# Two edits to a fused retention, spectral and gated MLP kernel: the sign in the narrowing of weights, and seven block products in the first layer's u half

## The chip, the cores and the metric

The kernel runs on one core of a Trainium2 chip, in one launch. The time is device microseconds (us). A core has five engines with queues of their own: TensorE (PE in the rows; PEld is its weight load), VectorE (DVE), ScalarE (ACT), GpSimd (POOL), and SyncE (SP), which here only issues DMAs. An engine takes its instructions strictly in the order in which they were written for it, so an instruction that waits holds up all that stand behind it on that engine.

## The reference, cut to what matters

Two batches, 768 tokens, 512 features, everything in fp32. Retention with a decaying state gives x. Then:

```python
theta = x @ w_theta                                   # spectral part
y = w_tok_r @ (x*cos(theta)) + w_tok_i @ (x*sin(theta))   # over tokens
u = x + y
x2 = u + max(u @ w_ch, 0)
h = gelu_tanh(x2 @ w_in)                              # 512 -> 1024
u, v = h[..., :512], h[..., 512:]
v = layernorm(v) * g_ln
out = x2 + (u * (w_sg @ v + b_sg)) @ w_out            # w_sg over tokens
```

The weights of `w_theta`, `w_tok_*`, `w_ch`, `w_in` and `w_out` reach the kernel as 64-bit floats and are narrowed to fp32 on the chip.

## The kernel before, in words

The kernel keeps activations with features on the 128 partitions and tokens along the free axis. Tokens form three column groups g: group 0 is batch 0's first 512 tokens, group 1 is batch 1's, group 2 the last 256 of both. A feature tile e (or f, d) is one of four blocks of 128. So an activation tile is 128x512.

TensorE multiplies in a reduced format (fp32r), so each fp32 operand is split in a high and a low part (`split_hi` on ScalarE, `split_lo` on VectorE), and a product is made of three matmuls, high by high, low by high and high by low (`terms3`). A 512-deep layer for one output tile (`layer`, `up_v`) is therefore 4 x 3 = 12 matmuls of 128x512.

Twelve chunks of 128 tokens go through `retention` (scores, mask, outer product, state) and `theta` (angle, sine, cosine, transposes), then the token mixing (`mix_main`, `mix_rest`). After that come `channels` (w_ch), `up_v` and `up_u` (the two halves of w_in with `gelu`), `norm` and `norm_tile` (layer norm of v), `gate_tile` (w_sg), and the last layer. For groups 0 and 1 the last layer runs by Strassen and Winograd's scheme: its 2x2 blocks (two halves of the depth, two halves of the output, two groups) take seven block products in place of eight. `sum_weights` and `sum_tokens` form the sums and differences of blocks that it needs and split them, `seven` issues the products, and `finish_four` adds them up. One block product is 2 x 3 = 6 matmuls of 128x512, and there are two per scheme entry (j = 0, 1).

`weight(k)` loads 128x1024 64-bit words. Narrowing one takes: on ScalarE a Copy of the high words times 2^-112 (L403), on VectorE a right shift of the low words (L412), then two SCALAR_TENSOR_TENSOR operations (L423): the high words shifted left by three or-ed in, and the sign bit of the high words or-ed in. There are 19 weights. The first two (`W_THETA`) live in the homes of `xb` and `xa`; the others pass through two raw buffers.

The program's order is written out by hand: each operation is recorded with its engine, and the table `ORDER`, a list of the operations' numbers, with start times from a small planner, decides in which order each engine's instructions are emitted and which buffer each gets. Before TensorE's first real work, and in planned gaps, the kernel puts matmuls of zeros or of the identity, read from `state` and `ident` (`keep_warm`). Their results are not used.

Of the kernel before, what the change touches and what calls it, by code (L numbers as in the profile page):

```python
# [10 lines left out]
F32 = mybir.dt.float32  # L11
# [20 lines left out]
REBIAS = 2.0**-112  # L32

# [29 lines left out]
class Plan:  # L63
# [160 lines left out]
def retention_spectral_gmlp(  # L224
# [153 lines left out]
    def weight(k, prio, eng=dve, after=()):  # L378
# [19 lines left out]
        def words(hi):  # L398
# [5 lines left out]
                out=words(1).bitcast(F32), in_=words(1).bitcast(F32), func=AF.Copy, scale=REBIAS  # L404
# [15 lines left out]
        for scalar, op in ((3, ALU.logical_shift_left), (-0x80000000, ALU.bitwise_and)):  # L420
            dve(
                1024,
                lambda scalar=scalar, op=op: V.scalar_tensor_tensor(  # L423
                    out=words(0), in0=words(1), scalar=scalar, in1=words(0),
                    op0=op, op1=ALU.bitwise_or,
                ),
                prio=prio,
                r=[(raw, 1)],
                w=[(raw, 0)],
            )  # L430
# [408 lines left out]
    def channels(g, e, prio):  # L839
# [9 lines left out]
        dve(512, relu, ps=True, r=[t], w=x_keys(g, e), prio=prio)  # L849
        split_x(x2hl, g, e, prio)  # L850

    def gelu(t, o, prio):

        s = Buf()
        act(
# [561 lines left out]
```

## Time and profile before

| | us |
|---|---|
| median of 3 runs | 370.33 (369.91 to 370.38) |
| the profiled execution, its own time | 370.23 |
| its span, first to last instruction | 368.5 |
| TensorE busy | 363.0 |
| VectorE busy | 290.1 |
| ScalarE busy | 178.6 |
| the PE part of the chain of work that ended last | 95% of the span |

The span is what the rows show, and 1.7 us of the execution's time lies around it. Busy time of an engine is the union of its instructions. The chain of work that ended last goes back from the last instruction, at each step to what released it, so its pieces add up to the span.

### The profile page before, as it was taken

Reading aid. Unit: us, or ns where it says so; the run is one execution under the profiler, and the core shown is the slowest. Engines: PE = TensorE matmul, PEld = TensorE weight load, DVE = VectorE, ACT = ScalarE, POOL = GpSimd, SP = SyncE. Lnnn points to the kernel's source line nnn. Section 1 sums busy time; section 2 is a strip of 40 time slices with the busy share of each in tenths; the row PEclk is TensorE's granted clock in tenths of the full one; section 3 lists DMA queues with packets and bytes.
Section 4 is the critical chain, followed back from the end, with each engine's and each line's share of the span. In section 5 each row is a group of like instructions: output and inputs, shape, how many; then the busy total and the mean of one; then the engine's idle time right before and its main releaser. Section 6 shows DMA issues by size and latency. Waiting matters only on the chain.

```text
span 368.5 us, 5764 instructions
## 1 busy us (share of the span) xinstructions
PE 363.0 (99%) x2364; PEld 311.7 (85%) x2364; DVE 290.1 (79%) x441; ACT 178.6 (48%) x298; POOL 10.8 (3%) x18
## 2 busy tenths in 40 slices
PE   8899999999999999999999999999999999999996
PEld 7788888788998988889988888888888889988885
DVE  3999999998886885775786434897999596899984
ACT  2767987742543566634343212437493744314300
POOL 1021010030001000000000000000000000000000
PEclk9999999999999999999999999999999999999999
DMA  7999990233433121414160000000000000000134
GB/s 306 410 413 407 410 384 6 88 141 121 166 114 116 34 84 34 166 30 161 68 223 6 2 0 0 2 1 0 0 2 0 0 2 1 3 0 2 58 114 171
DMA packets 10346, 39.08 MB, mean 106 GB/s; under 512 B 1360, under 2 KB 2384, under 8 KB 7888
## 3 DMA queue, kind: packets, MB, share of 16 engines
q1 hardware_dynamic: 10176, 38.67, 27.7%
q8 instruction: 18, 0.29, 0.3%
q10 hardware_dynamic: 144, 0.05, 0.1%
q14 instruction: 8, 0.07, 0.1%
HBM read 35.57 MB, written 3.15 MB: 105 GB/s over the span
## 4 chain that ended last, share of the span: by engine, by line
PE 95%; DMA 4%; DVE 0%; SPq 0%; issue 0%
PE banks L311 93%; DMA b<-qkv 3%; PE banks L716 1%; DMA dec<-decays 1%; DVE b L1231 0%; SPq L457 0%
## 5 line engine op out<-in xcount | busy, mean ns | idle before, releaser
L311 PE MATMUL banks<-b,b 128*128 128x512 f32 (+2 forms) x1776 | 327.3, 351 | 0.0
L311 PEld LDWEIGHTS banks<-b,b 128*128 128x128 f32 (+1 forms) x1776 | 276.4, 183 | 46.0 <-issue 1.2
L331 ACT ACTIVATE b<-b 128x512 fp32r<-128x512 f32 (+1 forms) x71 | 56.0, 815 | 67.4 <-DVE b L423 23.5
L337 DVE TENSOR_TENSOR b<-b,b 128x512 fp32r<-128x512 f32 (+1 forms) x71 | 62.4, 898 | 15.4 <-ACT b L331 9.2
L423 DVE SCALAR_TENSOR_TENSOR b<-b 128x1024 int32<-128x1024 int32 x32 | 38.8, 1224 | 0.8 <-ACT b L403 0.3
L331 ACT ACTIVATE b<-xa 128x512 fp32r<-128x512 f32 (+1 forms) x26 | 17.1, 670 | 25.4 <-DVE xa L845 15.9
L403 ACT ACTIVATE b<-b 128x1024 f32<-128x1024 f32 x16 | 18.6, 1160 | 11.6 <-DMA b<-wts 8.6
L857 ACT ACTIVATE b<-banks 128x512 f32<-128x512 f32 x24 | 13.7, 589 | 15.0 <-PE banks L311 15.0
L337 DVE TENSOR_TENSOR b<-xa,b 128x512 fp32r<-128x512 f32 (+1 forms) x26 | 19.1, 743 | 1.7 <-ACT b L331 1.6
L311 PE MATMUL banks<-b 64*128 64x128 f32 (+1 forms) x352 | 19.3, 256 | 0.8 <-DMA b<-qkv 0.8
L875 ACT ACTIVATE b<-b 128x512 f32<-128x512 f32 x24 | 14.7, 625 | 10.8 <-DVE b L865 10.8
L311 PEld LDWEIGHTS banks<-b 64*128 64x128 f32 (+1 forms) x352 | 17.1, 165 | 3.0 <-DMA b<-qkv 1.1
L865 DVE SCALAR_TENSOR_TENSOR b<-b,banks 128x512 f32<-128x512 f32 x24 | 15.9, 680 | 4.1 <-ACT b L857 4.1
L881 DVE SCALAR_TENSOR_TENSOR b<-b,banks 128x512 f32<-128x512 f32 x24 | 16.4, 682 | 2.6 <-ACT b L875 2.5
L724 DVE TENSOR_TENSOR b<-banks,b 128x1024 f32<-128x1024 f32 x12 | 14.7, 1223 | 3.9 <-ACT b L707 2.2
L526 ACT ACTIVATE b<-b,dec 128x64 f32<-128x64 f32 x56 | 14.1, 335 | 7.4 <-DMA b<-qkv 7.4
L503 DVE TENSOR_TENSOR b<-banks,causal 128x512 f32<-128x512 f32 x24 | 15.8, 686 | 1.7 <-PE banks L311 1.7
L412 DVE TENSOR_SCALAR b<-b 128x1024 int32<-128x1024 int32 x16 | 11.4, 717 | 4.2 <-DMA b<-wts 4.2
L331 ACT ACTIVATE b<-xb 128x512 fp32r<-128x512 f32 (+1 forms) x13 | 8.4, 663 | 12.3 <-DVE xb L845 8.7
L1036 DVE SCALAR_TENSOR_TENSOR b<-banks,gcol,brow 128x512 f32<-128x512 f32 x12 | 8.9, 749 | 5.5 <-PE banks L311 5.5
L845 DVE SCALAR_TENSOR_TENSOR xa<-banks,xa 128x512 f32<-128x512 f32 x8 | 5.5, 690 | 8.0 <-PE banks L311 7.9
L311 PE MATMUL banks<-b,state 64*64 64x128 f32 x160 | 10.9, 275 | 0.0
(66 smaller groups left out, 193.2 us busy)
## 6 DMA issues: line engine op xcount, KB each, us to landing
b<-wts SPq DMA_DIRECT2D x16, 1024.0 KB, 4.9
b<-qkv SPq DMA_DIRECT2D x24, 512.0 KB, 11.1
out<-b SPq DMA_DIRECT2D x11, 256.0 KB, 2.1
b<-wsg SPq DMA_DIRECT2D x9, 256.0 KB, 7.0
xa<-wts SPq DMA_DIRECT2D x2, 1024.0 KB, 11.2
xb<-wts SPq DMA_DIRECT2D x1, 1024.0 KB, 8.3
brow<-bvec SPq DMA_DIRECT2D x1, 384.0 KB, 11.4
dq<-qdecays SPq DMA_DIRECT2D x1, 256.0 KB, 6.4
```

The lines of the kernel that those rows point to most:

```text
L311: nc.tensor.matmul(out=o, lhsT=l, rhs=r, start=start, stop=stop, skip_group_check=more)
L331: act(words, lambda: A.activation(out=hi(), in_=src(), func=AF.Copy), prio=prio, r=r, **k)
L337: lambda: E.tensor_tensor(out=lo(), in0=src(), in1=hi().bitcast(F32), op=ALU.subtract),
L403: lambda: A.activation(out=words(1).bitcast(F32), in_=words(1).bitcast(F32), func=AF.Copy, scale=REBIAS),
L423: lambda scalar=scalar, op=op: V.scalar_tensor_tensor(out=words(0), in0=words(1), scalar=scalar, in1=words(0), op0=op, op1=ALU.bitwise_or,),
L503: V.tensor_tensor(out=ap(at[i])[:, h * 512 + lo : h * 512 + hi].rearrange("p (n t) -> p n t", n=n), in0=ap(sc[h])[:, lo:hi].rearrange("p ( ...
L526: A.activation(out=v, in_=v, func=AF.Copy, scale=dk[:, h : h + 1])
L724: V.tensor_tensor(out=z2, in0=ap(tp)[:, None, :].to_broadcast([P, 2, 512]), in1=z2, op=ALU.mult)
L857: lambda: A.activation(out=ap(s), in_=ap(t), func=AF.Square),
L865: lambda: V.scalar_tensor_tensor(out=ap(s), in0=ap(s), scalar=1.0 / GA, in1=ap(t), op0=ALU.add, op1=ALU.mult),
L875: lambda: A.activation(out=ap(s), in_=ap(s), func=AF.Tanh, scale=GA * GC),
L881: lambda: V.scalar_tensor_tensor(out=ap(o), in0=ap(s), scalar=1.0, in1=ap(t), op0=ALU.add, op1=ALU.mult),
```

## The change

There are two edits, and with them a new order.

The narrowing: ScalarE's Copy becomes a parametric relu with the same scale and alpha = 2^32. A negative word is so multiplied by a further 2^32, which sets one bit of its exponent field; the left shift by three moves that bit to the sign's place. The second SCALAR_TENSOR_TENSOR goes.

The first layer: the u half of w_in for groups 0 and 1 (eight layers of 12 matmuls) is now formed by `seven` as well, with a new function `up_four` that adds up the parts and calls `gelu`. Group 2 keeps `up_u`. `sum_weights` and `sum_tokens` are called for it.

```diff
-                out=words(1).bitcast(F32), in_=words(1).bitcast(F32), func=AF.Copy, scale=REBIAS
+                out=words(1).bitcast(F32), in_=words(1).bitcast(F32), func=AF.Prelu, scale=REBIAS,
+                alpha=SIGN_UP,
...
-        for scalar, op in ((3, ALU.logical_shift_left), (-0x80000000, ALU.bitwise_and)):
-            dve(
-                1024,
-                lambda scalar=scalar, op=op: V.scalar_tensor_tensor(
-                    out=words(0), in0=words(1), scalar=scalar, in1=words(0),
-                    op0=op, op1=ALU.bitwise_or,
-                ),
+        dve(
+            1024,
+            lambda: V.scalar_tensor_tensor(
+                out=words(0), in0=words(1), scalar=3, in1=words(0),
+                op0=ALU.logical_shift_left, op1=ALU.bitwise_or,
+            ),
...
+    def up_four(j, ws, ts, prio):
+        z, x, y, u, v = seven(W_INU, x2hl, ws, ts, j, prio)
+        for g, f, part in ((0, j, z), (1, j, x), (0, 2 + j, y), (1, 2 + j, v)):
...
+                t = v if part is v else Buf()
+                dve(
+                    512,
+                    lambda t=t, part=part: V.tensor_tensor(
+                        out=ap(t), in0=ap(part), in1=ap(u), op=ALU.add
+                    ),
...
+            gelu(t, gu[g, f], prio, ps=part is z)
...
+    ws = sum_weights(W_INU, t - 8)
+    ts = sum_tokens(lambda g, d: (lambda: x_tile(g, d), x_keys(g, d)), t - 4)
+    for f in range(NP):
+        up_u(2, f, t)
+    for j in range(2):
+        up_four(j, ws, ts, t)
...
 ORDER = [
-    56, 58, 57, 85, 86, 59, 0, 114, 113, 60, 141, 142, 63, 62, 64, 61, 741, 87, 66, 7, 90, 88, 169,
+    48, 50, 49, 78, 77, 51, 105, 106, 0, 52, 161, 133, 55, 54, 56, 53, 189, 82, 57, 58, 134, 79, 6,
...
```

The whole of `ORDER` is new (972 operations in place of 935). Three places of it matter below.

First, TensorE at the program's start, before: scores, outer products and attend of chunks 0 to 2. `ident` rows are the unused matmuls; the rows begin behind chunk 0's scores; b_100, b_108 and b_121 hold q and k of chunks 1 to 3, b_98, b_102 and b_106 k and v of chunks 0 to 2; b_126 and b_166 are masked scores; 128x512 rows are the first angle.

```order
L311 MATMUL banks<-ident 128x128 x2
L311 MATMUL banks<-b_98 64x64 x8
L311 MATMUL banks<-b_100 128x128 x8
L311 MATMUL banks<-b_126,b_98 64x128 x8
L311 MATMUL banks<-ident 128x128 x2
L716 MATMUL banks<-ident,xa_86 128x128 x4
L311 MATMUL banks<-b_102 64x64 x8
...
L311 MATMUL banks<-b_108 128x128 x8
L311 MATMUL banks<-b_106 64x64 x8
L311 MATMUL banks<-b_121 128x128 x8
...
L311 MATMUL banks<-b_235,b_179 128x512 x2
```

The same place now. Here b_102, b_105, b_123, b_121 and b_139 hold q and k of chunks 1, 2, 3, 4 and 5, and b_100 and b_107 k and v of chunks 1 and 2.

```order
L314 MATMUL banks<-ident 128x128 x2
L314 MATMUL banks<-b_98 64x64 x8
L314 MATMUL banks<-ident 128x128 x2
L314 MATMUL banks<-b_126,b_98 64x128 x8
L314 MATMUL banks<-b_102 128x128 x8
L314 MATMUL banks<-b_100 64x64 x8
L314 MATMUL banks<-b_105 128x128 x8
...
L314 MATMUL banks<-b_121 128x128 x8
L719 MATMUL banks<-ident,xa_86 128x128 x8
L314 MATMUL banks<-b_123 128x128 x8
L314 MATMUL banks<-b_139 128x128 x8
L314 MATMUL banks<-b_269,b_173 128x512 x2
```

Two more scores and one more chunk's transposes now stand ahead of the first angle. On SP's queue the first weight (xb) moved from sixth to eighth, behind both loads of chunk 2, and `gcol` and four gate weights went from among the first 33 loads to later places.

Second, VectorE between the channel tiles and the first layer, before (L845 is the relu of a channel tile, L337 a low part).

```order
L845 SCALAR_TENSOR_TENSOR xa_87<-banks,xa_87 128x512
L337 TENSOR_TENSOR b_1873<-xb,b_1873 128x512
L337 TENSOR_TENSOR b_1855<-xb,b_1855 128x512
L412 TENSOR_SCALAR b_1834<-b_1834 128x1024
L845 SCALAR_TENSOR_TENSOR xa_86<-banks,xa_86 128x512
```

And now, where L848 is the relu, L1098 a difference of token blocks, and L340 a low part.

```order
L848 SCALAR_TENSOR_TENSOR xa_87<-banks,xa_87 128x512
L1098 TENSOR_TENSOR b_1913<-xa_87,xa_86 128x512
L848 SCALAR_TENSOR_TENSOR xa_86<-banks,xa_86 128x512
L1098 TENSOR_TENSOR b_1928<-xa_87,b_1913 128x512
L340 TENSOR_TENSOR b_1857<-xb,b_1857 128x512
L1098 TENSOR_TENSOR b_1931<-xa_87,xa_86 128x512
L340 TENSOR_TENSOR b_1875<-b_1557,b_1875 128x512
L340 TENSOR_TENSOR b_1946<-b_1931,b_1946 128x512
L340 TENSOR_TENSOR b_1948<-b_1913,b_1948 128x512
L848 SCALAR_TENSOR_TENSOR xa_86<-banks,xa_86 128x512 x2
```

The differences stand among the channel tiles' relus; b_1948 and b_1946, the low parts of the first difference of blocks, are what the first of the seven products reads. On TensorE those products follow the channel tiles of groups 1 and 0; the four channel tiles of group 2 follow the first two products.

Third, VectorE between the last layer norm (it ends with L955, now L958) and the gate tiles, before.

```order
L955 SCALAR_TENSOR_TENSOR rstd<-mv,rstd 128x4
L865 SCALAR_TENSOR_TENSOR b_2515<-b_2515,banks 128x512
L881 SCALAR_TENSOR_TENSOR b_2552<-b_2452,banks 128x512
L881 SCALAR_TENSOR_TENSOR b_2552<-b_2515,banks 128x512
L1075 TENSOR_TENSOR b_2556<-b_1834,b_1780 128x512
L337 TENSOR_TENSOR b_2580<-b_2343,b_2580 128x512
```

And now.

```order
L958 SCALAR_TENSOR_TENSOR rstd<-mv,rstd 128x4
L340 TENSOR_TENSOR b_2592<-b_2420,b_2592 128x512
L340 TENSOR_TENSOR b_2597<-b_2420,b_2597 128x512
L340 TENSOR_TENSOR b_2152<-b_1483,b_2152 128x512
L340 TENSOR_TENSOR b_2465<-b_2273,b_2465 128x512
L340 TENSOR_TENSOR b_2434<-b_2268,b_2434 128x512
L1039 SCALAR_TENSOR_TENSOR b_2691<-banks,gcol_75,brow 128x512
L340 TENSOR_TENSOR b_2662<-b_2594,b_2662 128x512
L340 TENSOR_TENSOR b_2667<-b_2594,b_2667 128x512
L340 TENSOR_TENSOR b_2695<-b_2565,b_2695 128x512
L340 TENSOR_TENSOR b_2671<-b_2565,b_2671 128x512
```

The last four rows are group 1's normalised v, low parts, behind a row that reads the third gate tile of group 0 (L1039). On TensorE the last `up_v` of group 1 now stands directly ahead of group 0's four gate tiles; before, six layers of `up_u` stood between. Group 2's first gate tile follows group 0's four and is the first to read those low parts.

## Rows read from the trace of the kernel before

**Rows 1.** The page: busy time, and TensorE's granted clock in 40 slices, in tenths.

```profile
PE 363.0 (99%) x2364; PEld 311.7 (85%) x2364; DVE 290.1 (79%) x441; ACT 178.6 (48%) x298; POOL 10.8 (3%) x18
...
PEclk9999999999999999999999999999999999999999
```

**Rows 2.** The chain that ended last, in order of time: start, us, what.

```profile
16.56 30.70 PE banks L311 x384
...
49.68 8.20 PE banks L311 x36
...
130.49 234.79 PE banks L311 x1188
...
365.30 0.42 DVE b L1231
```

**Rows 3.** Timeline of TensorE from 4 to 19 us: start, duration, what.

```profile
4.80 1.16 PE L311 MATMUL banks<-b 64*128 64x128 f32 x16
5.89 0.71 PE L311 MATMUL banks<-ident 128*128 128x128 f32 x4
6.66 1.78 PE L311 MATMUL banks<-b 128*64 128x64 f32 x32
...
9.39 0.71 PE L311 MATMUL banks<-ident 128*128 128x128 f32 x4
10.26 0.66 PE L716 MATMUL banks<-ident,xa 128*128 128x128 f32 x4 [0.15 <-DVE xa L622]
10.84 0.69 PE L311 MATMUL banks<-b 128*64 128x64 f32 x16
...
13.50 0.49 PE L311 MATMUL banks<-ident 128*128 128x128 f32 x2
14.15 1.78 PE L311 MATMUL banks<-b 64*128 64x128 f32 x32 [0.16 <-DMA b<-qkv]
16.56 1.16 PE L311 MATMUL banks<-b 64*128 64x128 f32 x16 [0.64 <-DMA b<-qkv]
```

**Rows 4.** Timeline of all engines from 6 to 18 us.

```profile
6.52 1.28 DVE L503 TENSOR_TENSOR b<-banks,causal 128x512 f32<-128x512 f32 x2
8.47 2.02 ACT L526 ACTIVATE b<-b,dec 128x64 f32<-128x64 f32 x8 [5.97 <-DMA b<-qkv]
11.57 1.20 ACT L403 ACTIVATE xb<-xb 128x1024 f32<-128x1024 f32 x1 [0.56 <-DMA xb<-wts]
12.80 2.91 DVE L423 SCALAR_TENSOR_TENSOR xb<-xb 128x1024 int32<-128x1024 int32 x2
15.75 1.14 ACT L331 ACTIVATE b<-xb 128x1024 fp32r<-128x1024 f32 x1 [0.88 <-DVE xb L423]
17.42 1.22 DVE L337 TENSOR_TENSOR b<-xb,b 128x1024 fp32r<-128x1024 f32 x1
```

**Rows 5.** Groups by line and shape: count, busy us, mean ns, idle before.

```profile
L423 DVE SCALAR_TENSOR_TENSOR b<-b 128x1024 int32<-128x1024 int32 x32 | 38.8, 1224 | 0.8 <-ACT b L403 0.3
L337 DVE TENSOR_TENSOR b<-b,b 128x512 fp32r<-128x512 f32 x43 | 28.6, 686 | 5.3 <-ACT b L331 5.3
L331 ACT ACTIVATE b<-b 128x512 fp32r<-128x512 f32 x43 | 25.7, 623 | 30.8 <-DVE b L1043 16.0 <-DVE b L1095 9.2 <-PE banks L311 4.0
L311 PEld LDWEIGHTS banks<-b,b 128*128 128x128 f32 x1584 | 266.2, 189 | 44.2 <-ACT b L526 0.3
L1332 ACT ACT_TABLE_LOAD x1 | 1.3, 1283 | 1.2 <-PEq L1407 1.2
L966 ACT ACTIVATE b<-b,rstd 128x512 f32<-128x512 f32 x12 | 9.5, 807 | 2.3 <-DVE rstd L955 2.3
L954 DVE SCALAR_TENSOR_TENSOR rstd<-rstd 128x4 f32<-128x4 f32 x9 | 1.5, 162 | 0.3
```

**Rows 6.** Busy time of each engine by stretch (PE, PEld, DVE, ACT, ...).

```profile
17.00:60.00 43.00, 43.00 (x445) 36.30 (x441) 41.69 (x56) 34.02 (x73) 4.94 (x4) 1.00 0.90 360
...
130.00:240.00 110.00, 110.00 (x563) 94.32 (x562) 71.19 (x95) 45.66 (x67) 0.00 (x0) 1.00 0.17 61
```

More of the change, by code (lines that the diff above doesn't have):

```diff
@@ L32 @@
 REBIAS = 2.0**-112
+SIGN_UP = 2.0**32
 W_THETA, W_MAIN, W_REST, W_CH, W_INV, W_INU, W_OUT = 0, 2, 8, 11, 13, 15, 17
@@ L419, in weight @@
         )
-        for scalar, op in ((3, ALU.logical_shift_left), (-0x80000000, ALU.bitwise_and)):
-            dve(
-                1024,
-                lambda scalar=scalar, op=op: V.scalar_tensor_tensor(
-                    out=words(0), in0=words(1), scalar=scalar, in1=words(0),
-                    op0=op, op1=ALU.bitwise_or,
-                ),
[L427 to L430, printed above, removed]
+        dve(
[4 more added lines that the diff above has]
+            ),
+            prio=prio,
+            r=[(raw, 1)],
+            w=[(raw, 0)],
+        )
         h, l = wp[k]
@@ L850, in channels, with gelu @@
         split_x(x2hl, g, e, prio)
-    def gelu(t, o, prio):
+    def gelu(t, o, prio, ps=True):
         s = Buf()
@@ L857, in gelu @@
             lambda: A.activation(out=ap(s), in_=ap(t), func=AF.Square),
-            ps=True,
+            ps=ps,
             r=[t],
@@ L867, in gelu @@
             ),
-            ps=True,
+            ps=ps,
             r=[t],
@@ L883, in gelu @@
             ),
-            ps=True,
+            ps=ps,
             r=[t, s],
@@ L1104, in sum_tokens, with seven @@
         return res
-    def seven(base, src, hl, ws, ts, j, prio):
+    def seven(base, hl, ws, ts, j, prio):
         z, w, x, y = (bank() for _ in range(4))
@@ L1172, in store @@
         dma(256, put, r=[o], prio=prio)
+    def up_four(j, ws, ts, prio):
+        z, x, y, u, v = seven(W_INU, x2hl, ws, ts, j, prio)
+        for g, f, part in ((0, j, z), (1, j, x), (0, 2 + j, y), (1, 2 + j, v)):
+            if f % 2 == 0:
+                gu[g, f], gu[g, f + 1] = halves()
+            t = part
+            if part is not z:
+                t = v if part is v else Buf()
[4 more added lines that the diff above has]
+                    ),
+                    ps=part is not v, r=[part, u], w=[t], prio=prio,
+                )
+            gelu(t, gu[g, f], prio, ps=part is z)
     def finish_four(j, ws, ts, prio):
-        z, x, y, u, v = seven(W_OUT, None, ghl, ws, ts, j, prio)
+        z, x, y, u, v = seven(W_OUT, ghl, ws, ts, j, prio)
         def add(o, a, b, r, **k):
@@ L1269, in retention_spectral_gmlp @@
         weight(W_INU + k, t - 10 + 5 * k)
-        weight(W_INV + k, t - 7 + 5 * k)
+        weight(W_INV + k, t + 30 + 5 * k)
     for g in range(3):
@@ L1274, in retention_spectral_gmlp @@
             t += 2.7
+    ws = sum_weights(W_INU, t - 8)
+    ts = sum_tokens(lambda g, d: (lambda: x_tile(g, d), x_keys(g, d)), t - 4)
+    for f in range(NP):
+        up_u(2, f, t)
+        t += 2.7
+    for j in range(2):
+        up_four(j, ws, ts, t)
+        t += 9.5
     for g in (0, 2, 1):
@@ L1281, in retention_spectral_gmlp @@
             norm_tile(g, q, t + 1)
-        for f in range(NP):
-            up_u(g, f, t)
-            t += 2.7
     dma(384, lambda: nc.sync.dma_start(out=brow, in_=bvec), w=["brow"], prio=t - 20)
@@ L1296, in retention_spectral_gmlp @@
         weight(W_OUT + k, t + 20 + 5 * k)
-    for g in (2, 0, 1):
+    for g in (0, 2, 1):
         for f in range(NP):
```

96 rows, old and new, of the table ORDER are left out of this document.

## The prediction

> **What bounds the kernel now.** I read the page first, then the chain that ended last, then TensorE's timeline at the start and last the busy time by stretch. TensorE is busy for 363.0 of 368.5 us at a granted clock of 1.0, its higher level of 2.4 GHz, in every slice [rows 1]. Busy alone proves little, so the chain decides: from 16.56 us to its last matmul at 365.3 it runs along TensorE and names no wait on another engine, and only 0.42 us of VectorE follows [rows 2]. A stretch of it gives the price of one matmul: 36 of 128x512 in 8.20 us, 227.8 ns each [rows 2]. VectorE is at 41.69 of 43 us from 17 to 60 us, but TensorE did not wait for it; from 130 to 240 us it has 38.8 of 110 us to spare [rows 6]. So time goes in three ways only: fewer matmuls, less waste before 16.56, or new waits.
>
> Before 16.56 TensorE is not full. The unused matmuls of the identity and the DMA waits show it: real work ends at 5.89 and goes on at 6.66, ends at 9.39 and goes on at 10.26, 13.50 to 14.15, and 15.93 (14.15 + 1.78) to 16.56 [rows 3]. That is 0.77 + 0.87 + 0.65 + 0.63 = 2.92 us without real work.
>
> **The change part by part.** *The products.* Eight layers of 12 matmuls go, and 14 block products of 6 come: 96 - 84 = 12 matmuls of 128x512 less, 12 x 227.8 ns = 2.73 us [rows 2]. TensorE is the chain, so this comes off the end, if nothing new waits.
>
> Each of these matmuls has its own weight load, of 189 ns on average, and PEld is busy for 85% of the span [rows 1, 5]. The Trainium skill (Perfetto Trace Analysis, Identifying the Most-Contended Engine) says that matmul occupancy is no good measure of how near TensorE is to its peak and that the weight loads' busy share is. By the loads the 12 matmuls would give 12 x 189 ns = 2.27 us in place of 2.73. I go by the start-to-start spacing, which holds the load and whatever else paces a matmul.
>
> *VectorE's third operation.* 19 operations of 1224 ns go, 23.3 us [rows 5]. Most stand in the stretch in which VectorE is full, but TensorE waits for none of them after 16.56, so directly they give nothing. What they do give is freedom at the start (next point). Prelu in Copy's place: the trace shows no Prelu. The nearest row, Copy with a scale, takes 1.20 us [rows 4]; I take the same, bounds 0.6 less and 1.2 more (a second pass). ScalarE is idle about half the time, and the first weight below has 0.6 us of room, so even the upper bound costs some 0.6 us once.
>
> *What `up_four` adds.* On VectorE: 4 weight sums and 4 low parts, 8 token sums and 8 low parts, 4 adds in `both`, 6 adds in `up_four`: 34 x 0.686 = 23.3 us, what the narrowing gave back, but now between 130 and 240 us, into 38.8 us of idle time [rows 5, 6]. On ScalarE 4 + 8 high parts and 4 copies: 16 x 0.62 = 10 us into 64 us of idle time there. The `gelu` passes only change where they read. Cost on the path: zero, if the operands of the products are early enough. The tightest place is the first product. Its two operands' low parts stand six passes behind the relu of the second channel tile of group 0 (third pair of order rows, its second place). That tile ends two channel tiles, 2 x 12 x 0.228 = 5.5 us, before the product; relu and six passes are 7 x 0.63 = 4.4 us (two masks in a row took 1.28 [rows 4]), so about 1 us of room. Behind it four channel tiles of group 2, 10.9 us, cover the rest: 19 passes, 12 us, up to the latest operand of the next products, less the 1 us of room ahead and 2.7 us of the two first products. I take 0; bounds 0 and 3 us.
>
> *The start.* The order puts the first weight's load behind chunk 2's two loads, and more chunk work ahead of the first angle. Landings before: the fourth load by 8.4, the weight (after 256 KB for dq) by 11.57, two loads later 14.15, then 16.56 [rows 3, 4]: 2.55 us for 1 MB, and one step of 2.41 us for 0.5 MB. So now q and k of chunk 1 land at 8.4, of chunk 2 at 10.3, its k and v at 11.6, the weight at 14.1, chunk 4's q and k between 15.4 and 16.5, then one load per 1.3 us. TensorE: scores 0 as before to 5.89; the same 0.77 us until VectorE has faded v; outer product to 7.3; attend 0 needs both masks, which end at 6.52 + 1.28 = 7.80, so 0.6 us of filler; from 7.9 attend 0 (1.0), scores 1 (1.1), outer 1 (0.5), scores 2 (1.1, its data landed at 10.3), attend 1 and 2 (2.05 each), outer 2 (0.5) follow with their data there, to 16.3. Then scores 4, a wait of 0 to 0.2 us. Waste 0.77 + 0.6 + 0.1 = 1.5 us for 2.92 us: gain 1.4 us. Behind it come transposes of two chunks and scores 3 and 5, to 20.4 us, when the first angle starts. Is the weight there? Landed 14.1, Prelu 1.2, one operation of 1.46 (half of 2.91), high part 1.14, low part about 1.22 [rows 4] make 19.2, and about 0.6 us of VectorE's other passes stand between: 19.8, so 0.6 us early. With the second operation it would be 21.3 and late by 0.9: this is where the removed operation pays. Bounds of this term: a gain of 1.9 us (waste 1.0) and a loss of 1 us (the slow load step falls ahead of the weight and Prelu takes two passes). Behind it the loads stay ahead: one chunk load per 1.3 us against some 4 us of work per chunk.
>
> *The rest.* Switches between shapes change in number by a few, each some 0.1 to 0.2 us by the attend and score rows; I take 0, bounds 0.3 either way. The tail behind the last matmul, 0.42 us of VectorE and the store, has the same code.
>
> Sum against the profiled execution: 370.23 - 2.73 - 1.4 = 366.1 us. That execution lies 0.10 us under the median of 370.33, so the same figure serves for the median.
>
> **The rivals.** *The start gives nothing (367.5 us).* If the first angle waits for its weight or for a load, only the products remain: 370.23 - 2.73 = 367.5. For it: the room is 0.6 us, less than the slow load step of 1.1 us beyond the normal pace. Against: scores of three later chunks stand ahead and take up such a slip.
>
> *The last normalisation is late (368 to 370 us).* The last `up_v` of group 1 now ends where group 0's four gate tiles begin, 4 x 18 x 0.228 = 16.4 us before group 2's gate tile that reads it; before, six layers, 16.4 us more, lay between. Its path: gelu four passes, statistics and Newton steps of 14 x 0.162, together about 6 us, ScalarE's four scalings with high parts 4 x (0.81 + 0.62) = 5.7 [rows 5], then low parts that stand behind a row that reads the third gate tile, done at 12.3: 12.5 + 0.7 + 4 x 0.63 = 15.7. Room 0.7 us, and 2 more for batch 1's second half of that tile. If VectorE is 2 to 4 us late, as it may be with other work between, TensorE waits that long: 368 to 370.
>
> *The sums are in the way (371.7 us).* Slower than before. If the token and weight sums do not run beside the channel tiles but behind the last of groups 0 and 1, then 24 passes, 24 x 0.686 = 16.5 us, meet a cover of 10.9 us, and TensorE waits 5.6 us at the first layer's second set of products: 366.1 + 5.6 = 371.7. It decides from the point where the passes ahead of the products take more than those 10.9 us. For it: strict order on VectorE, where a relu that waits for TensorE holds up the sums behind it. Against: half of the sums stand ahead of the last relu.
>
> *Prelu forces table loads (372.5 us).* The one table load of the trace took 1.283 us [rows 5]. If Prelu were not in the loaded set, each narrowing would need a load there and one back, 2.57 us. From 17 to 60 us ScalarE is busy 34.0 of 43 us and narrows five weights: 34.0 + 12.8 = 46.8, some 4 us over; with 2.57 us at the first weight, 6.4 us, so 372.5. The Trainium skill (ScalarE: Activation LUTs, Table sets: the hidden batching unit) states that functions are loaded as sets and names copy and relu, not the parametric relu, among those that come with every set. Against: the built program still has one table load, ahead of all activations, as the trace of before has.
>
> **How the numbers follow.** Forecast, both gains within 0.8 us: 0.63 (365.3 to 366.9). Start without gain: 0.14. Late normalisation: 0.14, of which 0.05 end above 369.6. Sums in the way: 0.05. Table loads: 0.04. About 0.2%, 0.74 us, is what a measurement of this kernel can tell from no change. So faster 0.63 + 0.14 + 0.09 = 0.86, same 0.05, slower 0.09. The range reaches from 365.2 (gains of 2.73 and 1.9 and 0.3 for switches) to 368.8, which takes in the start without gain and the smaller half of the late normalisation.
>
> **What would show it.** Right: 1116 matmuls of 128x512 in place of 1128 at the same spacing; the chain on TensorE from about 16.5 us on without a wait; the first angle near 20.4 us, with six scores and two chunks' transposes ahead of it; one table load; Prelu near 1.2 us; VectorE fuller from 130 to 240 us and emptier from 17 to 60. Wrong: a wait of TensorE on a low part ahead of the first angle, at the first layer's products, or at group 2's first gate tile, or a spacing other than 228 ns.

## The result, and the profile after

The changed kernel takes 366.85 us (median of 4 runs, 366.21 to 367.32) against 370.32, a ratio of 0.9908, 95% interval 0.989 to 0.9925. It is faster by 3.5 us; the forecast was 366.1 in a range from 365.2 to 368.8. The profiled execution took 367.32 us with a span of 365.6, so it is the slowest of the four. Over all eight runs (four more stand below) the median is 366.5.

The page of the changed kernel, its busy line, answers to [rows 1]: VectorE as busy as before, ScalarE 7.9 us more, 14 matmuls fewer.

```profile
PE 361.2 (99%) x2350; PEld 310.4 (85%) x2350; DVE 290.6 (79%) x456; ACT 186.5 (51%) x314; POOL 12.4 (3%) x18
```

The chain that ended last (start, us, what) answers to [rows 2]. Its pace is the same, 8.20 us for 36 matmuls, and no wait stands in it from the first matmul on.

```profile
56.66 8.20 PE banks L314 x36
...
150.75 211.66 PE banks L314 x1080
...
362.43 0.42 DVE b L1251
```

The groups by line and shape (count, busy us, mean ns, idle before), answering to [rows 5]. 1116 matmuls of 128x512 instead of 1128. Prelu (now L406) takes 1153 ns for 1024 words, and there is one table load.

```profile
L314 PE MATMUL banks<-b,b 128*128 128x512 f32 x1116 | 258.1, 391 | 0.0
L426 DVE SCALAR_TENSOR_TENSOR b<-b 128x1024 int32<-128x1024 int32 x16 | 19.5, 1220 | 0.5 <-ACT b L406 0.3
L406 ACT ACTIVATE b<-b 128x1024 f32<-128x1024 f32 x16 | 18.4, 1153 | 11.0 <-DMA b<-wts 11.0
L1357 ACT ACT_TABLE_LOAD x1 | 1.3, 1283 | 1.2 <-PEq L1432 1.2
```

Busy time by stretch (PE, PEld, DVE, ACT, ...), answering to [rows 6]: VectorE went from 41.69 to 37.75 us in the first and from 71.19 to 82.98 in the second.

```profile
17.00:60.00 43.00, 43.00 (x478) 36.28 (x475) 37.75 (x51) 35.36 (x75) 6.05 (x5) 1.00 0.68 272
...
130.00:240.00 110.00, 110.00 (x580) 94.06 (x579) 82.98 (x117) 54.48 (x84) 0.12 (x1) 1.00 0.14 51
```

TensorE's timeline at the start (start, duration, what) answers to [rows 3]. Here is the one surprise.

```profile
3.96 1.49 PE L314 MATMUL banks<-ident 128*128 128x128 f32 x6
5.37 2.08 PE L314 MATMUL banks<-b 64*128 64x128 f32 x16
7.38 0.71 PE L314 MATMUL banks<-ident 128*128 128x128 f32 x4
...
9.27 1.09 PE L314 MATMUL banks<-b,b 128*64 128x128 f32 x16
...
19.77 2.06 PE L314 MATMUL banks<-b 64*128 64x128 f32 x32
21.75 3.04 PE L314 MATMUL banks<-b,b 128*128 128x512 f32 x12
```

The first scores take 2.08 us where they took 1.16 [rows 3]. The profile's record of TensorE's clock begins, at 1.0, at 7.31 us of this span and at 4.12 us of the span of before; ahead of that point identity matmuls start 0.213 us apart, behind it 0.111, so it is the step from 1.2 to 2.4 GHz. The first angle (the first 128x512 matmuls) starts at 21.75 us, forecast 20.4. From there to VectorE's last pass is 362.43 - 21.75 = 340.68 us; before it was 365.30 - 19.70 = 345.60.

### The profile page after: what moved, and what is told of

The parts are those of the page before. It is cut to its first block, busy times and chain, and to the rows that moved or that the text cites. A ratio compares the mean times of both kernels' runs of the same rounds, so it can differ in the third digit from the quotient of the medians.

```text
span 365.6 us, 5779 instructions
## 1 busy us (share of the span) xinstructions
PE 361.2 (99%) x2350; PEld 310.4 (85%) x2350; DVE 290.6 (79%) x456; ACT 186.5 (51%) x314; POOL 12.4 (3%) x18
## 4 chain that ended last, share of the span: by engine, by line
PE 99%; DVE 0%; issue 0%
PE banks L314 97%; PE banks L719 1%; DVE b L1251 0%; DVE state L272 0%; DVE halfpi L276 0%
## 5 line engine op out<-in xcount | busy, mean ns | idle before, releaser
L334 ACT ACTIVATE b<-b 128x512 fp32r<-128x512 f32 (+1 forms) x83 | 62.6, 786 | 51.9 <-DVE b L1098 17.0
L340 DVE TENSOR_TENSOR b<-b,b 128x512 fp32r<-128x512 f32 (+1 forms) x83 | 70.2, 870 | 14.5 <-PE banks L314 8.9
L406 ACT ACTIVATE b<-b 128x1024 f32<-128x1024 f32 x16 | 18.4, 1153 | 11.0 <-DMA b<-wts 11.0
L340 DVE TENSOR_TENSOR b<-xa,b 128x512 fp32r<-128x512 f32 (+1 forms) x26 | 18.7, 728 | 4.9 <-ACT b L334 4.9
L426 DVE SCALAR_TENSOR_TENSOR b<-b 128x1024 int32<-128x1024 int32 x16 | 19.5, 1220 | 0.5 <-ACT b L406 0.3
L529 ACT ACTIVATE b<-b,dec 128x64 f32<-128x64 f32 x56 | 14.1, 334 | 5.4 <-DMA b<-qkv 5.4
L684 DVE SCALAR_TENSOR_TENSOR b<-banks,b 128x512 f32<-128x512 f32 x12 | 8.3, 689 | 7.9 <-PE banks L314 4.8
L675 ACT ACTIVATE b<-banks 128x512 int32<-128x512 f32 x12 | 7.1, 590 | 14.3 <-PE banks L314 14.3
L969 ACT ACTIVATE b<-b,rstd 128x512 f32<-128x512 f32 x12 | 9.6, 808 | 8.5 <-DVE rstd L958 8.5
L884 DVE SCALAR_TENSOR_TENSOR b<-b,banks 128x512 f32<-128x512 f32 x18 | 12.2, 680 | 1.7 <-ACT b L878 1.3
L868 DVE SCALAR_TENSOR_TENSOR b<-b,banks 128x512 f32<-128x512 f32 x18 | 11.9, 679 | 1.0 <-ACT b L860 0.9
L860 ACT ACTIVATE b<-banks 128x512 f32<-128x512 f32 x18 | 10.4, 593 | 4.5 <-PE banks L314 3.7
```

Of the source, the lines that this page charges most:

```text
L334: act(words, lambda: A.activation(out=hi(), in_=src(), func=AF.Copy), prio=prio, r=r, **k)
L340: lambda: E.tensor_tensor(out=lo(), in0=src(), in1=hi().bitcast(F32), op=ALU.subtract),
L406: lambda: A.activation(out=words(1).bitcast(F32), in_=words(1).bitcast(F32), func=AF.Prelu, scale=REBIAS, alpha=SIGN_UP,),
L426: lambda: V.scalar_tensor_tensor(out=words(0), in0=words(1), scalar=3, in1=words(0), op0=ALU.logical_shift_left, op1=ALU.bitwise_or,),
L529: A.activation(out=v, in_=v, func=AF.Copy, scale=dk[:, h : h + 1])
L868: lambda: V.scalar_tensor_tensor(out=ap(s), in0=ap(s), scalar=1.0 / GA, in1=ap(t), op0=ALU.add, op1=ALU.mult),
```

## The experiments

Twelve kernels, in three sets of four, each set on one chip beside the kernel before (median 370.25 to 370.35 in every set). Two numbers are read from each profile: when the first angle starts, and how long it is from there to VectorE's last pass. They part what happens at the start from all the rest.

| kernel | median us (range) | ratio to before, 95% | clock rises | first angle | from there to the end |
|---|---|---|---|---|---|
| before | 370.3 | 1 | 4.12 | 19.70 | 345.60 |
| changed | 366.85 (366.21-367.32) | 0.989-0.9925 | 7.31 | 21.75 | 340.68 |
| changed again | 366.32 (366.27-366.96) | 0.9885-0.9912 | 5.09 | 20.77 | 340.65 |
| start alone | 369.19 (368.85-369.91) | 0.9963-0.9985 | 6.03 | 21.14 | 343.23 |
| layers back | 369.08 (368.9-369.75) | 0.9963-0.9982 | 4.96 | 20.79 | 343.37 |
| Prelu alone | 370.25 (369.79-370.46) | 0.999-1.0008 | 6.81 | 19.88 | 345.60 |
| third op, first weight | 367.12 (366.91-367.27) | 0.9903-0.9932 | 6.98 | 21.60 | 340.64 |
| third op, all weights | 369.49 (369.25-369.72) | 0.9971-0.999 | 4.18 | 21.18 | 343.43 |
| low part six times | 368.97 (368.88-371.34) | 0.9956-0.9998 | 4.79 | 20.65 | 343.34 |
| no unused matmuls | 366.41 (366.33-366.77) | 0.9886-0.9915 | 7.97 | 20.93 | 340.66 |
| no fillers | 366.30 (366.18-367.21) | 0.9893-0.9919 | 10.24 | 21.55 | 340.64 |
| no fillers, swap | 366.02 (365.99-366.11) | 0.9875-0.9906 | 4.13 | 20.45 | 340.69 |
| before, no unused matmuls | 370.26 (369.45-370.84) | 0.9991-1.001 | 9.83 | 19.82 | 345.62 |
| start alone, long narrowing | 375.55 (375.09-375.67) | 1.0131-1.0159 | 5.21 | 21.15 | 349.62 |

**The changed kernel again**, no edit.

> The changed kernel once more, unchanged. The forecast was 366.1 us, the median came out at 366.85, in single runs from 366.21 to 367.32. Theory A (the clock): the shortfall of 0.75 us is the moment at which TensorE's granted clock first reads 1.0. In the profile of before that was at 4.12 us of the span, in that of the changed kernel at 7.31 us, and the matmuls between ran at half pace. A expects runs spread over at least 0.8 us again, median 366.3 to 367.2, and in this profile the pair: if the granted clock rises near 4 us, the first angle at 20.2 to 20.8 us and a time of 365.9 to 366.4; if near 7 us, the first angle at 21.5 to 22.0 us and 367.0 to 367.5. Rival (the order): the later first angle belongs to the new order itself, whatever the clock; then the first angle stands at 21.6 to 21.9 us in any profile and the time does not follow the rise.

The clock rose at 5.09 us, and angle and time came out as theory A had them for an early rise: 20.77 us, and 366.31 in the profiled execution. The part behind the angle is the same to 0.03 us. TensorE's timeline, and below it the first weight's Prelu and low part:

```profile
3.95 1.38 PE L314 MATMUL banks<-ident 128*128 128x128 f32 x6
5.26 1.16 PE L314 MATMUL banks<-b 64*128 64x128 f32 x16
6.36 0.71 PE L314 MATMUL banks<-ident 128*128 128x128 f32 x4
...
8.25 1.09 PE L314 MATMUL banks<-b,b 128*64 128x128 f32 x16
...
16.07 1.76 PE L314 MATMUL banks<-b 128*64 128x64 f32 x32
...
20.77 3.02 PE L314 MATMUL banks<-b,b 128*128 128x512 f32 x12
```

```profile
15.36 1.21 ACT L406 ACTIVATE xb<-xb 128x1024 f32<-128x1024 f32 x1 [1.75 <-DMA xb<-wts]
...
19.27 1.26 DVE L340 TENSOR_TENSOR b<-xb,b 128x1024 fp32r<-128x1024 f32 x1
```

Both executions run the same 2350 matmuls in the same order. The one with the late rise is 0.1 us behind where the first scores start, 1.0 where they end (7.38 against 6.36), 1.0 at attend 0 (9.27 against 8.25) and 1.0 at VectorE's last pass (362.43 against 361.42). So all of the difference arises in the first scores, at half pace, and nothing behind them takes it back.

The weight landed 1.35 us later here than in the other execution (14.01), and its low part, done at 20.53, is first read at 21.33, the angle's third matmul: 0.8 us of room.

**The start alone.** The kernel before, narrowing shortened, its first 250 steps in the new order, layers as before.

```diff
-ORDER = [56, 58, 57, 85, ...]              # before's order
+ORDER = [<250 steps as in the changed kernel>, <the rest as before>]
-func=AF.Copy, scale=REBIAS                  # and two sign operations
+func=AF.Prelu, scale=REBIAS, alpha=2.0**32  # and one
```

> The kernel before with one operation fewer per weight (Prelu in Copy's place) and with its first 250 steps in the order of the changed kernel; the layers' eight products are as before. This is the start's term alone. Theory A: 370.3 less 0.4 (late rise of the clock) to 1.4 us (early rise): 368.9 to 369.9, with the first angle at 20.4 (early) to 21.8 us (late), and no wait of TensorE from 16.6 us on. Rival (all of the gain is the twelve matmuls): 370.1 to 370.5. Rival (the order in the middle, not the start, gained): 370.1 to 370.5 too, with a first angle at 20.4 and a wait or slower spacing later.

Within A's range: 1.1 us of gain. Behind the angle 345.60 - 343.23 = 2.37 us less is left to do, and the angle comes 1.44 us later in this execution.

**The layers back.** The changed kernel with the products taken out again.

```diff
-    up_four(j, ws, ts, t)
+    for g, f in ((0, j), (1, j), (0, 2 + j), (1, 2 + j)):
+        up_u(g, f, t)
```

> The changed kernel with the eight layer tiles of groups 0 and 1 in place of the fourteen products of the first layer, without their sums; start and narrowing stay as changed. This is the products' term alone. Theory A: 12 matmuls more at 227.8 ns, all on the end: 366.85 + 2.73 = 369.6 (369.2 to 370.1), and 1128 matmuls of 128x512. Rival (TensorE is paced by its weight loads, 189 ns each): 366.85 + 2.27 = 369.1. Rival (the 34 more VectorE passes of the products cost something on the path): less than 2 us more, 368.9 or under.

369.08 lies just under A's range (369.2 to 370.1) and at the rival's 369.1, so the times don't decide it; the traces do. Chain:

```profile
149.76 214.38 PE banks L312 x1092
...
364.16 0.42 DVE b L1249
```

The last stretch has 12 matmuls more than the changed kernel's and is 214.38 - 211.66 = 2.72 us longer; from the angle to the end it is 343.37 - 340.67 = 2.70. That is 225 ns for a matmul, not the 189 of its weight load.

**Prelu alone**, the kernel before with the second hunk of the diff above and its own order.

> The kernel before, in its own order, with Prelu in Copy's place and without the 19 operations; nothing else changed. Theory A (the removed operations give nothing by themselves, TensorE waits for none of them): 370.1 to 370.5, VectorE some 23 us less busy, the first angle still near 19.7 us (or 1.3 us later if the clock rises late). Rival (VectorE held TensorE up in small pieces in its fullest stretch, 17 to 60 us): 368.5 to 369.8, with a shorter time from the first angle to the last matmul than 345.6 us. Rival (Prelu takes two passes): VectorE's gain is lost on ScalarE, mean of Prelu above 2 us.

No change, though VectorE is 21.6 us less busy than before (page of this kernel):

```profile
PE 364.1 (99%) x2364; PEld 312.8 (85%) x2364; DVE 268.5 (73%) x422; ACT 177.5 (48%) x298; POOL 10.8 (3%) x18
```

The rise at 6.81 instead of 4.12 moved the angle by 0.18 us only.

**The third operation back, for the first weight and for all**, in the changed kernel:

```diff
+    if k == W_THETA:      # left out in the second kernel
+        dve(1024, lambda: V.scalar_tensor_tensor(out=words(0), in0=words(1), scalar=-0x80000000,
+            in1=words(0), op0=ALU.bitwise_and, op1=ALU.bitwise_or), ...)
```

> The changed kernel with VectorE's third operation back for the first weight alone (1.22 us, it ORs in a sign that is there already, so nothing else changes). The prediction held that the removed operation pays here: first angle's operand 0.6 us early without it, 0.9 late with it. By the two profiles of the changed kernel the low part ends 1.64 us ahead of its reader where the clock rose at 7.31 us (first angle at 21.75) and 0.24 us ahead where it rose at 5.09 (first angle at 20.77, the weight landed at 15.3 instead of 14.0). Theory A: a wait of 0 to 1.0 us at the first angle, on VectorE, by execution: first angle at 21.7 us in nearly every one, median 366.9 to 367.4 against 366.3 to 366.9 without it, and runs below 366.5 gone. Rival (TensorE's clock and the chunk loads alone set the first angle): unchanged, 366.3 to 366.9.

> The changed kernel with VectorE's third operation back for all 19 weights (23.3 us of VectorE), all else in the changed order. Theory A (the operation pays nothing where VectorE has room, but the new order has packed VectorE so that it has none in 17 to 60 us): 37.75 us of 43 busy in the profile of the changed kernel, some six weights there, 7.3 us more, so 45 of 43: waits of TensorE of 1 to 3 us in all between 20 and 60 us, 367.8 to 370. Rival (its removal is worth nothing, as in the kernel before): 366.3 to 367.2. Rival (it is worth all of the gain): 370 and more.

The first kernel came out as A had it, 0.6 us above the changed kernel's median of eight, but its profile does not show the cause: its clock rose late, and the low part was done at 21.70, in time. The second, in an execution with an early rise, does. Passes of VectorE that read TensorE's banks stand behind the operation (L637, which scales a chunk's retention result, starts at 19.03 us; the same pass, L625, starts at 17.75 in the kernel changed again). The scores ahead of the first angle take 2.43 us instead of 2.06, and go on right where these passes end. Then the low part ends at 21.82, and the angle's twelve matmuls take 3.32 us instead of 3.02. TensorE:

```profile
18.82 2.43 PE L316 MATMUL banks<-b 64*128 64x128 f32 x32
21.18 3.32 PE L316 MATMUL banks<-b,b 128*128 128x512 f32 x12
```

The greater waits stand behind this, at the second and third weight. Waits of TensorE (engine, line, awaited line, us, times, longest):

```profile
PE banks L316 <- DVE b L518: 0.9, 1, 0.9
PE banks L316 <- DVE b L696: 0.7, 1, 0.7
```

and VectorE's timeline at these places, where L438 is the operation put back, L518 a mask and L696 an angle's pass:

```profile
25.67 1.21 DVE L428 SCALAR_TENSOR_TENSOR xa<-xa 128x1024 int32<-128x1024 int32 x1
26.92 1.52 DVE L438 SCALAR_TENSOR_TENSOR xa<-xa 128x1024 int32<-128x1024 int32 x1
28.36 0.68 DVE L518 TENSOR_TENSOR b<-banks,causal 128x512 f32<-128x512 f32 x1
...
35.94 1.51 DVE L438 SCALAR_TENSOR_TENSOR b<-b 128x1024 int32<-128x1024 int32 x1
37.37 1.27 DVE L696 SCALAR_TENSOR_TENSOR b<-banks,b 128x512 f32<-128x512 f32 x2
```

What TensorE needs next is queued behind the operation. This kernel and the one changed again run the same 2350 matmuls in the same order. TensorE is level with that execution at chunk 4's scores (16.70 against 16.67 us), 0.6 us behind within the first angle, 1.7 behind the mask, 2.9 behind the angle's pass and 3.2 at the end; the last 0.3 come at 244.8 us, where a bank is copied out late (L1154, on ScalarE). From the angle to the end it is 343.43 - 340.67 = 2.8 us more.

**Start alone, with the long narrowing**: Copy and both sign operations, the new first 250 steps.

> The kernel before, with its own narrowing (Copy and both sign operations on VectorE), its layers, and the first 250 steps in the order of the changed kernel. With the shorter narrowing this order gave 369.2 against 370.3. Theory A (the removed operation is what makes that order possible): the waits of third_all come again (0.9 and 0.7 us at 29 and 38 us, on passes queued behind the third operation of the second and third weight) and the 1.1 us turn into a loss of 1 to 4 us: 371 to 374. Rival (the order alone gives the gain): 369.2 to 369.8. Rival (the order gives it at the start and loses only a part later): 369.8 to 371.

Slower still than A had it: 5.3 us above the kernel before, 6.4 above the same order with the short narrowing. The same two waits are there and two new ones later. So with the operation in place this order of the start is a loss. Waits of TensorE:

```profile
PE banks L312 <- DVE b L882: 1.2, 1, 1.2
PE banks L312 <- DVE b L338: 1.0, 1, 1.0
PE banks L312 <- DVE b L504: 0.9, 1, 0.9
PE banks L312 <- DVE b L682: 0.7, 1, 0.7
```

**A low part six times**, the one ahead of the first of the seven products:

```diff
     split(res[i, n], lambda i=i, t=t: ap(t[i]), 512, prio, [t[i]])
+    if (i, n) == (0, 0) and not again:      # the first call alone
...
+        for _ in range(5):
+            split_lo(
...
```

> The changed kernel with one low part ahead of the first of the seven products taken six times instead of once (same values), which puts five passes of 0.687 us, 3.4 us, on VectorE. In the profile that low part ended 0.69 us ahead of its reader. Theory A (the room at that place is 0.7 us and nothing behind it gives the rest back): TensorE waits 3.4 - 0.7 = 2.7 us there and the time rises by as much, 369.0 to 369.6. Rival (the room is larger, since VectorE idles ahead of it and would start earlier): a wait under 1.5 us. Rival (VectorE's lateness goes on to later readers): more than 2.7 us, above 369.8, with a second wait behind it.

TensorE waited 2.38 us, and the part behind the angle grew by 343.34 - 340.67 = 2.67. TensorE, then VectorE, in this kernel:

```profile
202.64 5.60 PE L315 MATMUL banks<-b,b 128*128 128x512 f32 x24
210.62 3.72 PE L315 MATMUL banks<-b,b 128*128 128x512 f32 x15 [2.38 <-DVE b L341]
```

```profile
205.64 4.92 DVE L341 TENSOR_TENSOR b<-b,b 128x512 fp32r<-128x512 f32 x7 [0.15 <-ACT b L335]
```

The two passes of the changed kernel, and where they stand:

```profile
206.77 1.29 DVE L340 TENSOR_TENSOR b<-b,b 128x512 fp32r<-128x512 f32 x2 [0.16 <-ACT b L334]
```

Seven passes in 4.92 us, where two took 1.29: 3.63 us more on VectorE. TensorE stopped ahead of the product's third matmul. In the changed kernel that one starts at 209.21 us, 1.15 after the two passes end (206.77 + 1.29 = 208.06). So 1.15 us fell into the room and about 2.5 reached the end. A had the size, with the median 0.03 us under its range, by two errors that cancel: the passes took more than 3.4 us, and the room is greater than its 0.7, which counts to the product's first matmul; one run of 371.34 stays unexplained.

**Unused matmuls.** All 13 out, then only the seven in the gaps (the fillers), then these and a swap: chunk 0's transposes ahead of chunk 4's scores.

```diff
-    for _ in range(6):
-        mm(warm[:, 0:P], states[0][:, 0:P], states[0][:, 0:P], True, True)   # first kernel only
-                keep_warm(idle[0], ...)                                       # in all
+                pass
```

> The changed kernel without the unused matmuls at the start (six before the first load has landed, seven in the first gaps), so TensorE's first matmul comes with the first data, near 4.6 us. Theory A (the later the granted clock rises, the later the first angle, about half a microsecond for each): the clock rises later than in the other profiles (4.1 to 7.3 us), at 8 us or more, the matmuls before it at half pace, first angle at 22 us or later, 367.5 to 369. Rival (the fillers themselves hold up the real work, the clock matters little): first angle at 20.8 to 21.7, 366.2 to 367.2.

Theory A fell: the latest rise so far, 7.97 us, and yet the angle at 20.93, 366.41, all four runs within 0.44 us. Its TensorE timeline:

```profile
4.64 3.23 PE L314 MATMUL banks<-b 64*128 64x128 f32 x32 [4.64 <-DMA b<-qkv]
8.18 1.09 PE L314 MATMUL banks<-b,b 128*64 128x128 f32 x16 [0.32 <-DVE b L506]
...
16.83 1.16 PE L314 MATMUL banks<-b 64*128 64x128 f32 x16 [0.21 <-DMA b<-qkv]
...
20.93 3.01 PE L314 MATMUL banks<-b,b 128*128 128x512 f32 x12
```

Real work starts 0.73 us sooner than behind the fillers (5.37), TensorE waits for a mask at 8.18 all the same, and what is left is chunk 4's load at 16.8 with 4.1 us of work up to the angle.

> The changed kernel with the six unused matmuls before the first data, but without the seven in the first gaps. Without all thirteen the clock rose latest of all profiles (7.97 us), and yet the first angle came at 20.93 us, since the scores began at 4.64 instead of 5.37: so the idea that a late rise alone makes a late first angle has fallen. New theory B: the unused matmuls between real ones hold those up when the clock is still at its lower level, and what is left as a floor is chunk 4's load, which lands at 16.5 to 16.8 us, with 4.1 us of work between it and the first angle. B expects scores 0 at 4.6 to 4.8, the first angle at 20.7 to 20.95, a wait on that load of 0.1 to 0.7 us, and 366.2 to 366.5 in all runs, spread under 0.6 us, whichever moment the clock rises. Rival (the early six matmuls also bring the clock up early, which pays): first angle under 20.6, 366.0. Rival (the fillers were needed to keep the clock): a fall of the clock between 5 and 9 us, first angle above 21.3, 366.8 or more.

Half right. Three runs are at 366.18 to 366.30, two at 367.1 and 367.2, so the spread did not go. The profiled one is of the latter; its clock rose at 10.24:

```profile
8.08 1.98 PE L314 MATMUL banks<-b,b 128*64 128x128 f32 x16 [0.31 <-DVE b L506]
9.99 2.97 PE L314 MATMUL banks<-b 64*128 64x128 f32 x48
...
21.55 3.01 PE L314 MATMUL banks<-b,b 128*128 128x512 f32 x12
```

Attend 0 at half pace took 1.98 us instead of 1.09, behind the last wait that could have absorbed it. So without fillers a late rise costs much only where it comes behind the start of attend 0, at about 8 us: with a rise at 4.13 (the swap, below) attend 0 started at 7.82 and with 7.97 at 8.18, most of the half pace ahead of it being hidden in the waits for VectorE. With the fillers, which stand in those waits, a rise at 7.31 us put attend 0 at 9.27. B was right that they hold real work up while the clock is low, and wrong that the moment of the rise does not matter without them.

> As no_fill, and with the transposes of chunk 0 (0.44 us, their operand is there at 14.9 us) ahead of the scores of chunk 4. Theory B (the load of chunk 4 is the floor): those transposes fill the wait, the first angle moves to 20.3 to 20.7, unless the first weight's low part holds it (it ends 20.5 where that weight lands at 15.4): 366.0 to 366.3, 0.1 to 0.3 us under no_fill. Rival (another limit at the same place): no change, or 0.2 us slower by the extra change of matmul shape.

366.02 us in four runs within 0.12 us, each faster than all eight of the changed kernel (on other chips). TensorE's timeline, L720 being the transposes:

```profile
15.64 0.64 PE L315 MATMUL banks<-b 128*64 128x64 f32 x16
16.20 0.66 PE L720 MATMUL banks<-ident,xa 128*128 128x128 f32 x4
16.79 1.16 PE L315 MATMUL banks<-b 64*128 64x128 f32 x16
...
20.45 3.06 PE L315 MATMUL banks<-b,b 128*128 128x512 f32 x12
```

The wait for chunk 4's load is filled, and the angle moves to 20.45. This is the fastest version here; how it does when the clock rises late, no profile here shows.

**The kernel before without unused matmuls**, the same edit as the first of these.

> The kernel before without any unused matmuls at the start. Theory B: in the order of before, loads set TensorE's pace up to 16.56 us (chunks of data land at 14.1 and 16.5), so neither the fillers nor the moment of the clock's rise reach the end: 370.1 to 370.5 and a spread as before; the first wait after the clock's rise is on a load. Rival (fillers cost in any order): 369.6 to 370.0. Rival (before needed them for its clock): over 370.7.

B held on the time, 370.26. The first wait behind the rise was one of 0.9 us on VectorE, though, not on a load. With its rise at 9.83 us the angle came 0.12 us later than with 4.12.

## Why the prediction was right

- *The products.* Forecast 2.73 us, shown 2.70 by the traces with and without them (2.6 between the medians). The Trainium skill (Perfetto Trace Analysis, Identifying the Most-Contended Engine) takes the weight loads' busy share as a measure of how close TensorE is to its peak; the estimate by the loads was 2.27, and the traces do not agree with it.
- *What `up_four` adds* was forecast at nothing, and TensorE waits nowhere for it. The room of the first product was forecast as about 1 us; its low parts end 1.15 us before the matmul that reads them. Five passes more there cost 2.4 to 2.7 us, so the mechanism of the rival with the sums in the way is real, and the room kept it off.
- *The start.* Forecast 1.4 us. Shown: 0.93 with a rise at 6.03 us (2.37 us of work moved ahead less 1.44 of a later angle); by the angle of the changed kernel, 2.37 - 1.07 = 1.30 with a rise at 5.09 and 2.37 - 2.05 = 0.32 with 7.31. The step that was off is "scores 0 as before to 5.89": it took the clock's rise of one execution as given. The order of before hid a late rise in its waits (6.81 and 9.83 us moved its angle by under 0.2 us). The new order has no load to wait for until chunk 4's, and the fillers stand in the wait for the masks, so a rise at 7.31 us reaches the end. In the two profiled executions this is the whole difference (367.32 and 366.31 us); that it also parts the other six runs, and so makes the median's shortfall of 0.75 us, is likely but not shown.
- *The first angle* was forecast at 20.4 us. A second size was off here: chunk 4's load was to land between 15.4 and 16.5 us and landed at 16.5 to 16.8, so that with an early rise (and without the third operation) the angle still stands at 20.65 to 20.79; only the swap brought it to 20.45. By the 2.37 us of the runs, 20.4 would have been a gain of 1.7, and 1.4 is an angle at 20.7. So the forecast's 1.4 is what an early rise gives, in part by luck: the load sets it, and not the waits that the forecast added up.
- *"This is where the removed operation pays."* Right in kind: nothing in the old order, 2.8 to 3 us in the new one, 6.4 with the layers unchanged. But the place was mis-sized. In the one profile that shows it the first weight accounts for 0.6 to 0.7 us (forecast 0.9), half of it ahead of the angle. More than 2 us are at the second and third weight, where the forecast took VectorE's stretch from 17 to 60 us to cost nothing.
- *Prelu* at 1.15 us as Copy, one table load: that rival is out.
- *The last normalisation.* The four low parts of group 1 end at 297.97 us and the first matmul that reads them starts at 300.67: the room of 0.7 and 2 us was right, and it was enough.
- *Small slips* of the working change nothing: 370.23 - 2.73 - 1.9 - 0.3 is 365.3 and not 365.2, 14.1 and the four passes behind it make 19.1 and not 19.2, and the two loads behind the first weight took 14.15 - 11.57 = 2.58 us and not 2.55.

Together, between the two profiled executions: 4.92 us less behind the angle (2.70 of products and 2.37 moved ahead, less 0.15; layers back and start alone, which differ in the order behind the first 250 steps, are 0.14 apart) and 2.05 us more ahead of it: 2.87, where the executions differ by 370.23 - 367.32 = 2.91.

## What to carry to other kernels

An operation that nobody waits for is worth nothing where it is removed and may be worth microseconds as room for another order: judge the two edits together, by putting the operation back into the new order. An order that fills its waits, with real or with unused matmuls, also gives up what absorbed the variation from one execution to the next, so a start must be worked out for an early and a late clock. To part a start from the rest, take from each profile the time at which a fixed instruction starts and the length from there to the end; here this agreed to 0.05 us where medians varied by 0.5.

## What the hardware showed that was not expected

TensorE's clock rose at 4.12 to 10.24 us of the span in 14 profiles, in the same kernel at 5.09 and 7.31, though its first matmul stood at 1.23 or 1.24 us in each of them but the two without unused matmuls. The Trainium skill (TensorE: Matmul & The Clock Gate, Part 1: The HAM clock gate) says that the window by which the chip judges TensorE's activity runs by itself, so that the same kernel has more or fewer slow matmuls from run to run. The profiles agree that the number varies; why, none of them shows.

In the eleven profiles with the new start the first weight landed at 15.3 to 15.5 us where the clock rose before 5.3 us, and at 14.0 to 14.2 where it rose at 6.0 or later; the load behind it landed at 16.5 to 16.8 in all. What ties the two is open.
